# Re-ranking the planned order of a fused window-attention and two-MLP kernel, with one DRAM tile per later token block

## Chip, cores and metric

The kernel runs on one core of a Trainium2 chip. The metric is the device time of the launch in microseconds (us), lower is better; the times before are 829.63, 829.7 and 830.26 us, with a median of 829.7 us.

## What is computed

The inputs are q, k and v for 4 sequences of 576 tokens, 8 heads of 64; in all 2304 tokens of model width 512. Attention looks back over a window of 64 tokens. Two MLPs of inner width 2048 follow, the first with a squared relu, the second with a leaky relu.

```python
mask = (rel >= 0) & (rel < 64)
scores = np.where(mask, (1 / np.sqrt(D)) * (q @ k.T), -1e9)
x = softmax(scores) @ v                     # 2304 x 512
r = np.maximum(x @ moe_w_in, 0.0)
y = (s * (r * r) + b) @ moe_w_out           # 2304 x 512
h = y @ moe2_w_in
out = np.maximum(0.01 * h, h) @ moe2_w_out
```

## The kernel before

**Attention.** The tokens are 18 tiles of 128. Tiles 0 to 7 (the early ones, which feed token blocks 0 and 1) go through `add_attention`, tiles 8 to 17 through `add_later`. A later tile runs: load of q and k halves (`qk`, L241), load of v into a buffer `vs` of pool "big" (L247), scores on TensorE (`sc`, L272), ScalarE's copy of the scores into the same buffer (L337), the mask on VectorE (L346), a row maximum (L355, L358), eight exponentials on ScalarE (L363), normalising on VectorE (L369 to L372), a transpose on TensorE (`tp`, L378), its two copies on VectorE (L386, L390), the product with v on TensorE (`xps`, L403), a copy of each half to `pt` (ScalarE L412, VectorE L414), and a store of `pt` to the DRAM tile `xdr` (L568). The pool "big" holds two buffers.

**First MLP.** Tokens are cut into five blocks (four of 512, one of 256), the inner width into 16 chunks. A step is one block and one chunk: 12 matmuls `hps` (L680), then ScalarE's `r` (L692), VectorE's `r` (L694), ScalarE's `gh` (L697), VectorE's `gl` (L699), and 12 matmuls `acc` (L715) that add to four PSUM banks. Every fp32 operand is split into a high and a low part, so each product is three matmuls. The steps run as block 0 with chunks 0 to 7, block 1 with all chunks, block 0 with chunks 8 to 15, then blocks 2, 3 and 4. Where block 0 is finished, VectorE adds the sum stored earlier to each bank (`part`, L738) before the next block may use the bank. Blocks 2 to 4 read their x back from `xdr` (`xl`, L573) and split it (L578, L580). The weights of each chunk are rounded and split by ScalarE and VectorE (`add_weights`, L602 to L641).

**Second MLP.** It runs as seven products per pair of quarters instead of eight, over three blocks of 768 tokens (L1052). Its combined weights are made ahead, during the first MLP, in units u0, u1, ...: one load of 1 MB into a buffer `raw2` of the same pool "big" (L820), ScalarE's first copy into `flt2` (L602), VectorE's roundings (L604 to L616), sums (L847), low parts (L876, L868), ScalarE's high parts (L874, L866), and six stores to the DRAM tile `w1dr` (L884). The pool "tmp" of `flt2` and `pt` holds two buffers.

**The order.** Class `Order` plans the whole program before it is emitted. Each piece of work is given an engine, a reckoned time, a key, the pieces it follows, the buffers it takes and uses, and for a transfer a further `delay` until it counts as landed. Each engine takes the lowest key that is ready in the plan; the emitted order is then fixed, and on the chip each engine works through its own queue in that order and waits at the head of it. All the large loads and stores stand in SyncE's queue (SP). When a buffer is handed on, the next user waits for the transfers out of it. A step's keys are its number plus offsets; attention tiles, weight chunks and weight units have keys set by tables. Where the plan sees TensorE idle near the start, products of zeros are put in (`product_of_zeros`, L1284).

Of the kernel before, what the change touches and what calls it, by code (L numbers as in the profile page):

```python
# [9 lines left out]
F32 = mybir.dt.float32  # L10
# [5 lines left out]
P = 128  # L16
# [110 lines left out]
def kernel(  # L127
# [39 lines left out]
    xdr = dramp.tile([P, KD, T], F32, name="xdr")  # L167
# [37 lines left out]
    half = KF // 2  # L205
# [210 lines left out]
    def add_later(i, key):  # L416
# [9 lines left out]
        for g in range(2):  # L426
            add(name("sc", g), "pe", 480, key - 6, lambda g=g: scores(i, g, "t"),
# [3 lines left out]
        for r in range(2):  # L431
            add(name("tb", r), "act", 375, key - 5.7, lambda r=r: take_own(i, r),
                [name("sc", 1), name("both")], use=[("sc", i, r), ss])
            add(name("to", r), "dve", 660 if mask_of(i) else 330, key - 4.87, lambda r=r: take_before(i, r),
                [name("tb", r), ("masks",)], use=[("sc", i, r), ss])
# [5 lines left out]
        add(name("norm"), "dve", 1050, key - 3, lambda: normalise_all(i),  # L441
            [name("exp", h) for h in range(H)], use=[("sm", i), ss])
        add(name("tp"), "pe", 480, key - 2.96, lambda: transpose_all(i),
            [name("norm"), ("masks",)], [("t", "tp", i)], [ss])
        for n in range(2):
            add(name("tt", n), "dve", 640, key - 5.69, lambda n=n: part_keys(i, n),
# [5 lines left out]
        add(name("pv"), "pe", 1150, key - 1, lambda: values_all(i), [name("bank")],  # L452
            [("h", "xt", i, 1)], [("xt", i, 0), ss, pt])
        add(name("xo", 0), "act", 400, key - 5, lambda: leave_half(i, 0), [name("pv")],
            use=[("xt", i, 0), pt])
        add(name("xo", 1), "dve", 350, key - 5, lambda: leave_half(i, 1), [name("xo", 0)],
# [27 lines left out]
    def add_attention(i, b, t0, key):  # L484
# [12 lines left out]
        for n, room in enumerate((rq, rk)):  # L497
            add(name("lqk", n), "sp", 1000, key - 5.93, lambda n=n: load_qk(i, n),
                [name("lqk", 0)] if n else [], room, delay=1900)
        add(name("lv"), "sp", 1600, key - 2.25, lambda: load_v(i),  # L500
# [7 lines left out]
        for g in range(2):  # L508
            add(name("sc", g), "pe", 700, key - 5.82, lambda g=g: scores(i, g, sc),
# [5 lines left out]
            for j in range(4):  # L515
                add(name("mm", g, j), "dve", 172, key - 5.47, lambda g=g, j=j: mask_max(i, g, j),
                    [name("sc", g)] + ([name("mm", 0, 0)] if g + j else after_v) + [("masks",)],
                    first if g + j == 0 else (), [("sc", i, j % 2), ss, ("sm", i)])
                add(name("exp", g, j), "act", 390, key - 2.81, lambda g=g, j=j: exponent(i, g, j),
                    [name("mm", g, j)], use=[ss, ("sm", i)])  # L520

            if i < 2:
                add(name("inv", g), "dve", 360, key - 3.4, lambda g=g: invert(i, g, g + 1),
                    [name("exp", g, j) for j in range(4)], use=[("sm", i)])
            elif g == 0:
                add(name("inv", 0), "dve", 360, key - 3.4, lambda: invert(i, 0, 2),
# [891 lines left out]
```

## Time and profile before

| | us |
|---|---|
| median of three runs | 829.7 |
| the profiled execution | 827.88 |
| its span | 826.1 |
| TensorE busy in the span | 814.0 |
| VectorE busy | 624.0 |
| ScalarE busy | 414.6 |

The granted clock was 0.999 over the span (1.00 is the level of 2.4 GHz). All times of rows count from the start of the span. Attention and the first MLP take up to about 475 us, the second MLP the rest. A row of a timeline or of the chain begins with its start and its length; what stands in brackets is the idle time of the engine just before it and what ended that.

### The profile page before, as it was taken

How to read it: one execution, taken by the hardware profiler on the slowest of the kernel's cores; microseconds unless marked ns; L12 is line 12 of the kernel's file. 1: busy time of each engine (PE TensorE's matmuls, PEld its weight loads, DVE VectorE, ACT ScalarE, POOL GpSimd, SP SyncE). 2: the span in 40 equal slices, each digit the busy share in tenths (PEclk: the TensorE clock that was granted, in tenths of full speed). 3: DMA queues.
4: the chain of work that ended last, by engine and by line, in shares of the span. 5: the costliest groups of instructions: out<-in, count | busy, mean ns of one | idle time of the engine just before them, and what ended most of it. 6: DMA issues, size and time to landing. Idle time of an engine off the chain costs nothing.

```text
span 826.1 us, 14490 instructions
## 1 busy us (share of the span) xinstructions
PE 814.0 (99%) x5541; PEld 734.0 (89%) x5541; DVE 624.0 (76%) x1019; ACT 414.6 (50%) x880; POOL 4.5 (1%) x18
## 2 busy tenths in 40 slices
PE   8999999999989999999999999999999999999998
PEld 5778888888878887888889999999999999999998
DVE  6999997786877877778787857699366788455964
ACT  7999655355555454544446434256233365232443
POOL 2000000000000000000000000000000000000000
PEclk9999999999999999999999999999999999999999
DMA  8754543438666565657688399798887899878783
GB/s 327 282 190 145 168 170 131 140 109 274 185 238 201 201 218 162 217 181 235 212 279 281 127 315 353 257 322 279 292 268 257 269 304 306 272 253 262 254 265 112
DMA packets 84757, 192.32 MB, mean 233 GB/s; under 512 B 6992, under 2 KB 47952, under 8 KB 80720
## 3 DMA queue, kind: packets, MB, share of 16 engines
q1 hardware_dynamic: 84688, 191.39, 69.3%
q8 instruction: 44, 0.72, 0.4%
q14 instruction: 25, 0.20, 0.1%
HBM read 148.90 MB, written 42.47 MB: 232 GB/s over the span
## 4 chain that ended last, share of the span: by engine, by line
PE 90%; DVE 4%; ACT 2%; DMA 2%; issue 1%; ACTq 0%; SPq 0%
PE xps L1052 24%; PE acc L715 22%; PE hps L680 21%; PE zps L1052 12%; PE yps L1052 6%; PE sc L272 2%; PE xps L403 1%; PE warm L1284 1%; DMA w1dr<-raw 1%; DMA xdr<-pt 1%; DVE s L284 1%; DVE tmp L612 1%; ACT s L290 1%; DVE tmp L616 1%; PE xps L328 1%
## 5 line engine op out<-in xcount | busy, mean ns | idle before, releaser
L715 PE MATMUL acc<-gh,wh 128*128 128x512 f32 (+1 forms) x320 | 117.3, 372 | 1.2 <-ACT gh L697 1.2
L680 PE MATMUL hps<-xh,wh 128*128 128x512 f32 (+1 forms) x324 | 117.0, 368 | 0.5 <-ACT wh L635 0.5
L680 PE MATMUL hps<-xl,wh 128*128 128x512 f32 (+1 forms) x324 | 116.4, 367 | 0.0
L715 PE MATMUL acc<-gh,wl 128*128 128x512 f32 (+1 forms) x320 | 116.1, 368 | 0.0
L1052 PE MATMUL xps<-x2h,ws 128*128 128x384 f32 x384 | 105.8, 334 | 0.0
L952 DVE TENSOR_TENSOR g2s<-g,g2s 128x768 fp32r<-128x768 f32 x84 | 80.2, 955 | 29.6 <-ACT g2s L949 28.6
L1052 PE MATMUL xps<-g2s,ws 128*128 128x384 f32 x576 | 101.8, 334 | 0.0
L1075 ACT ACTIVATE part<-xps 128x384 f32<-128x384 f32 x90 | 43.9, 490 | 114.9 <-PE xps L1052 114.2
L1052 PEld LDWEIGHTS xps<-g2s,ws 128*128 128x128 f32 x576 | 100.0, 188 | 0.1
L949 ACT ACTIVATE g2s<-g 128x768 fp32r<-128x768 f32 x84 | 70.8, 847 | 58.1 <-PE xps L1052 37.5
L692 ACT ACTIVATE r<-hps 128x512 f32<-128x512 f32 (+1 forms) x80 | 44.4, 555 | 100.7 <-PE hps L680 100.2
L715 PE MATMUL acc<-gl,wh 128*128 128x512 f32 (+1 forms) x320 | 85.5, 371 | 0.0
L694 DVE SCALAR_TENSOR_TENSOR r<-r,sbt 128x512 f32<-128x512 f32 (+1 forms) x80 | 55.6, 695 | 36.0 <-ACT r L692 35.4
L680 PE MATMUL hps<-xh,wl 128*128 128x512 f32 (+1 forms) x324 | 79.7, 368 | 0.0
L697 ACT ACTIVATE gh<-r,sbt 128x512 fp32r<-128x512 f32 (+1 forms) x80 | 54.2, 677 | 37.4 <-DVE r L694 37.0
L680 PEld LDWEIGHTS hps<-xh,wh 128*128 128x128 f32 x324 | 61.1, 189 | 11.4 <-ACT wh L635 1.1
L715 PEld LDWEIGHTS acc<-gh,wh 128*128 128x128 f32 x320 | 60.3, 189 | 11.9 <-ACT gh L697 1.7
L680 PEld LDWEIGHTS hps<-xl,wh 128*128 128x128 f32 x324 | 61.1, 189 | 10.2 <-DVE xl L580 0.6
L1052 PEld LDWEIGHTS xps<-x2h,ws 128*128 128x128 f32 x384 | 70.1, 188 | 0.0
L715 PEld LDWEIGHTS acc<-gh,wl 128*128 128x128 f32 x320 | 60.4, 189 | 9.7
L699 DVE SCALAR_TENSOR_TENSOR gl<-r,sbt,gh 128x512 fp32r<-128x512 f32 (+1 forms) x80 | 55.5, 693 | 15.2 <-ACT gh L697 15.1
L715 PEld LDWEIGHTS acc<-gl,wh 128*128 128x128 f32 x320 | 56.7, 189 | 10.4 <-issue 0.7
(106 smaller groups left out, 1369.7 us busy)
## 6 DMA issues: line engine op xcount, KB each, us to landing
ws<-w1dr SPq DMA_DIRECT2D x84, 512.0 KB, 4.5
ws<-w2dr SPq DMA_DIRECT2D x84, 512.0 KB, 4.5
raw<-in_w SPq DMA_DIRECT2D x31, 1024.0 KB, 4.9
w1dr<-raw SPq DMA_DIRECT2D x16, 512.0 KB, 4.3
w2dr<-raw SPq DMA_DIRECT2D x16, 512.0 KB, 4.5
qk<-in_qk SPq DMA_DIRECT2D x20, 320.0 KB, 4.0
out<-st SPq DMA_DIRECT2D x24, 192.0 KB, 4.1
qk<-in_qe SPq DMA_DIRECT2D x16, 256.0 KB, 7.5
```

Of the source, the lines that this page charges most:

```text
L272: nc.tensor.matmul(out=sc_t[i][r][D * a:D * a + D, p, c0:c1], lhsT=qk_t[i, g][D * r:D * r + D, pp, D * a:D * a + D], rhs=qk_t[k, g][D * r: ...
L284: nc.vector.tensor_tensor_reduce(out=s_t[i][:, g, j, :], in0=sc_t[i][j % 2][:, 2 * g + j // 2, :], in1=mask[:, mask_of(i), :], scale=-SCAL ...
L680: nc.tensor.matmul(out=hps_t[s][:, c0:c1], lhsT=w[:, 0, kk * P:kk * P + P], rhs=x[l, b][:, kk, c0:c1], start=(kk == 0 and j == 0 and part ...
L692: nc.scalar.activation(out=r, in_=hps_t[s], func=ACTF.Relu)
L694: nc.vector.scalar_tensor_tensor(out=r, in0=r, scalar=sbt[:, 0:1], in1=r, op0=ALU.mult, op1=ALU.mult)
L697: nc.scalar.activation(out=gh, in_=r, func=ACTF.Identity, bias=sbt[:, 1:2])
L699: nc.vector.scalar_tensor_tensor(out=gl, in0=r, scalar=sbt[:, 1:2], in1=gh.bitcast(F32), op0=ALU.add, op1=ALU.subtract)
L715: nc.tensor.matmul(out=acc_t[r, m], lhsT=three[j][0], rhs=three[j][1], start=(c == c0 and j == 0), stop=(c == c1 - 1 and j == 2))
L949: nc.scalar.activation(out=out, in_=in_, func=ACTF.Copy)
L952: nc.vector.tensor_tensor(out=out, in0=in_, in1=hi.bitcast(F32), op=ALU.subtract)
L1052: nc.tensor.matmul(out=out, lhsT=w_[:, wcut], rhs=x_, start=(opens and j == k == 0), stop=(j == n - 1 and k == 2), skip_group_check=not opens)
L1075: nc.scalar.activation(out=t, in_=bank_t[(*key, "x")], func=ACTF.Copy)
```

## The change

Keys are set anew for the later tiles, the early tiles, the steps, the weight chunks and the weight units, most of them by small amounts. `xdr` becomes one DRAM tile for each of the blocks 2, 3 and 4, so the loads of x read contiguous rows. In the plan, a unit's buffers count as used for another 930 ns after each of its stores (a new piece of work named "gone" that emits nothing), and the wait ahead of a store is 200 instead of 500 ns. The first product of each later pair in the second MLP is given a rank 2.5 products earlier. The zero products start with 5 instead of 4 and end after step 5 instead of 7; their number, counted in the emitted order, is 49 in both kernels. `half` keeps its value of 8.

```diff
-    xdr = dramp.tile([P, KD, T], F32, name="xdr")
+    xdr = {b: dramp.tile([P, KD, n], F32, name=f"xdr{b}") for b, n in enumerate(BLOCKS1) if b > 1}
...
-            add(name("sc", g), "pe", 480, key - 6, lambda g=g: scores(i, g, "t"),
+            add(name("sc", g), "pe", 480, key - 7.32, lambda g=g: scores(i, g, "t"),
...
-        add(name("max"), "dve", 800, key - 4.87, lambda: row_max(i),
+        add(name("max"), "dve", 800, key - 11.33, lambda: row_max(i),
...
-            add(name("exp", h), "act", 330, key + 3, lambda h=h: exponent_row(i, h),
+            add(name("exp", h), "act", 330, key + 8.74, lambda h=h: exponent_row(i, h),
...
-        nc.sync.dma_start(out=xl[0, b][:, :, :n].bitcast(F32), in_=xdr[:, :, t0:t0 + n])
+        nc.sync.dma_start(out=xl[0, b][:, :, :n].bitcast(F32), in_=xdr[b])
...
-            [("x", *r) for r in x], delay=9000 if b > 2 else 4000)
+            [("x", *r) for r in x], delay=3785.46 if b > 2 else 6398.4)
...
-        add(("e", s, 3), "dve", 60 + 600 * f, s + (-0.76 if s < 8 else -0.9), lambda: activate(s, 3),
+        add(("e", s, 3), "dve", 60 + 600 * f, s + (-13.55 if s < 8 else 0.69), lambda: activate(s, 3),
...
-    DUE = 500
+    DUE = 200.0
...
+            add((*name(kind), "gone"), "none", 0, key, lambda: None, [name(kind)], use=[raw, flt],
+                delay=929.73)
...
+            at = key + (-2.5 if i == 1 and p else j) * ms
+            add(name("p", i), "pe", 6 * MM, at, lambda i=i: product1(b, p, i),
...
-    WARM, BETWEEN = 4, 13
+    WARM, BETWEEN = 5, 13
...
-    add(("fill", 1), "none", 0, 0, end_fill, [("e", KF // 2 - 1, 0)])
+    add(("fill", 1), "none", 0, 0, end_fill, [("e", 5, 0)])
...
-                key = first_step[0, 2] + -10.0 + 2 * (i - IN_W)
+                key = first_step[0, 2] + -10.14 + 2.09 * (i - IN_W)
...
-        add_weights2(u, STEPS1 + (1 if u[1] else -10) + 0.1 * n, after)
+        add_weights2(u, STEPS1 + (1.17 if u[1] else -8.65) + 0.1 * n, after)
```

Three places in the emitted order follow. The first is SP's queue around tile 13 (its v goes into `vs_2615` before, into `vs_2587` now); `raw2_2262` and `raw2_2305` are the buffer of unit u2, `flt2` its scratch. Before:

```order
L573 DMA xl_2519<-xdr_99 128x4x512
L884 DMA w1dr_100<-flt2_2372 128x2x256
L884 DMA w1dr_100<-flt2_2372 128x256
L884 DMA w1dr_100<-raw2_2262 128x4x256 x2
L247 DMA vs_2615<-in_vl 128x768
L241 DMA qk_2646<-in_qk 128x640
```

Now:

```order
L890 DMA w1dr_102<-raw2_2305 128x4x256
L247 DMA vs_2587<-in_vl 128x768
L241 DMA qk_2618<-in_qk 128x640
L567 DMA xdr3_100<-pt_2538 512x1x128
L890 DMA w1dr_102<-raw2_2305 128x4x256
L241 DMA qk_2659<-in_qk 128x640
```

Tile 13's load stood behind all of u2's stores and took u2's buffer; now it stands ahead of the last of them and takes the buffer of tile 12.

The second is SP's queue around tile 11, where `raw2_1911` is unit u1's buffer and `vs_2260` is tile 11's. Now:

```order
L890 DMA w1dr_102<-raw2_1911 128x4x256
L755 DMA ydr_98<-st_2188 128x512
L890 DMA w1dr_102<-raw2_1911 128x4x256
L755 DMA ydr_98<-st_2203 128x512
L755 DMA ydr_98<-st_2245 128x512
L247 DMA vs_2260<-in_vl 128x768
L241 DMA qk_2283<-in_qk 128x640
```

Before, the buffer that u1 leaves went to u2's load, and tile 11 followed that:

```order
L884 DMA w1dr_100<-raw2_1899 128x4x256 x2
L820 DMA raw2_2262<-in_w2 128x2048
L247 DMA vs_2302<-in_vl 128x768
L241 DMA qk_2334<-in_qk 128x640
L568 DMA xdr_99<-pt_2245 512x1x128
```

Tile 11 now takes the buffer that u1's last two stores leave.

The third is ScalarE's queue behind tile 17's product (`pt_3407`, now `pt_3410`), with the first copies `flt2` of units u5 and u6 among the `r` and `gh` of the steps. Before:

```order
L412 ACTIVATE pt_3407<-xps_3417 128x256
L602 ACTIVATE flt2_3468<-raw2_3409 128x1024
L692 ACTIVATE r_3481<-hps_3459 128x512
L602 ACTIVATE flt2_3495<-raw2_3456 128x1024
L697 ACTIVATE gh_3482<-r_3481,sbt_97 128x512
```

Now:

```order
L412 ACTIVATE pt_3410<-xps_3419 128x256
L698 ACTIVATE r_3479<-hps_3459 128x512
L608 ACTIVATE flt2_3484<-raw2_3456 128x1024
L703 ACTIVATE gh_3480<-r_3479,sbt_97 128x512
L698 ACTIVATE r_3511<-hps_3486 128x512
L608 ACTIVATE flt2_3516<-raw2_3473 128x1024
L703 ACTIVATE gh_3512<-r_3511,sbt_97 128x512
```

Each first copy moved back by about one step, u5's from ahead of the first `r` to behind it, and u6's from ahead of the first `gh` to ahead of the second.

## Rows read from the trace of the kernel before

**Rows 1.** The page's first part, busy time by engine.

```profile
PE 814.0 (99%) x5541; PEld 734.0 (89%) x5541; DVE 624.0 (76%) x1019; ACT 414.6 (50%) x880; POOL 4.5 (1%) x18
```

**Rows 2.** Stretches: length, PE, PEld, DVE, ACT, POOL busy, clock, DMA, GB/s.

```profile
0.00:20.00 20.00, 16.60 (x251) 10.34 (x252) 13.21 (x73) 14.19 (x55) 4.51 (x18) 1.00 0.88 326
20.00:50.00 30.00, 28.36 (x355) 22.56 (x354) 29.41 (x83) 27.94 (x82) 0.00 (x0) 1.00 0.71 266
50.00:90.00 40.00, 39.77 (x351) 32.18 (x350) 39.07 (x79) 36.01 (x88) 0.00 (x0) 1.00 0.42 148
90.00:135.00 45.00, 45.00 (x200) 37.26 (x199) 43.42 (x51) 23.71 (x30) 0.00 (x0) 1.00 0.46 157
...
225.00:260.00 35.00, 32.91 (x293) 26.45 (x292) 27.51 (x51) 18.45 (x57) 0.00 (x0) 1.00 0.66 223
...
475.00:593.00 118.00, 118.00 (x681) 117.67 (x680) 83.59 (x107) 49.29 (x78) 0.00 (x0) 1.00 0.91 305
```

**Rows 3.** TensorE's waits from 60 to 475 us: total, times, longest.

```profile
PE tp L378 <- DVE vs L372: 2.1, 1, 2.1
PE acc L715 <- ACT gh L697: 1.2, 1, 1.2
```

**Rows 4.** The chain that ended last, 215 to 245 us: start, length, what.

```profile
221.34 1.23 DVE raw L868
...
222.59 7.99 DMA w1dr<-raw
...
230.68 0.40 ACT vs L337
...
238.64 0.63 PE tp L378 x4
...
241.32 1.06 PE xps L403 x48
242.38 0.88 PE sc L272 x32
```

**Rows 5.** ScalarE's timeline at tile 13.

```profile
230.68 0.66 ACT L337 ACTIVATE vs<-sc 128x256 f32<-128x256 f32 x2 [3.15 <-DMA w1dr<-raw]
```

**Rows 6.** The chain that ended last, 296 to 314 us.

```profile
303.14 7.09 DMA xdr<-pt
...
310.39 0.07 ACT flt L602
...
311.40 0.72 ACT gh L697
```

**Rows 7.** ScalarE's timeline behind tile 17.

```profile
302.92 1.11 ACT L602 ACTIVATE flt<-raw 128x1024 f32<-128x1024 f32 x1
307.40 0.60 ACT L692 ACTIVATE r<-hps 128x512 f32<-128x512 f32 x1 [3.36 <-PE hps L680]
```

**Rows 8.** VectorE's timeline at u4's last low part and tile 17's normalising.

```profile
292.05 1.22 DVE L868 TENSOR_TENSOR raw<-raw 128x1024 f32<-128x1024 f32 x1
...
296.56 0.69 DVE L372 TENSOR_TENSOR vs<-vs,sum 128x512 f32<-128x512 f32 x1
```

**Rows 9.** The page's DMA issues, whole span: count, KB each, median us to landing.

```profile
w1dr<-raw SPq DMA_DIRECT2D x16, 512.0 KB, 4.3
```

**Rows 10.** DMA issues from 200 to 245 us.

```profile
w1dr<-raw SPq DMA_DIRECT2D x2, 512.0 KB, 8.0
raw<-in_w SPq DMA_DIRECT2D x1, 1024.0 KB, 7.3
```

**Rows 11.** DMA issues from 285 to 330 us.

```profile
raw<-in_w SPq DMA_DIRECT2D x3, 1024.0 KB, 5.5
```

**Rows 12.** VectorE's and TensorE's timelines at block 0's third bank.

```profile
248.82 0.68 DVE L738 TENSOR_TENSOR part<-acc,part 128x512 f32<-128x512 f32 x1
249.89 0.39 PE L715 MATMUL acc<-gh,wh 128*128 128x512 f32 x1
```

**Rows 13.** The page's costliest groups: busy, mean ns, idle before and its releaser.

```profile
L699 DVE SCALAR_TENSOR_TENSOR gl<-r,sbt,gh 128x512 fp32r<-128x512 f32 (+1 forms) x80 | 55.5, 693 | 15.2 <-ACT gh L697 15.1
```

More of the change, by code (lines that the diff above doesn't have):

```diff
@@ L497, in add_attention @@
         for n, room in enumerate((rq, rk)):
-            add(name("lqk", n), "sp", 1000, key - 5.93, lambda n=n: load_qk(i, n),
+            add(name("lqk", n), "sp", 1000, key + (-6.93 if early else -6.81), lambda n=n: load_qk(i, n),
                 [name("lqk", 0)] if n else [], room, delay=1900)
-        add(name("lv"), "sp", 1600, key - 2.25, lambda: load_v(i),
+        add(name("lv"), "sp", 1600, key + (-2.57 if early else 5.03), lambda: load_v(i),
             [("lw", 0, KF - 1, 0, 2)] if i == IN_W else
@@ L508, in add_attention @@
         for g in range(2):
-            add(name("sc", g), "pe", 700, key - 5.82, lambda g=g: scores(i, g, sc),
+            add(name("sc", g), "pe", 700, key + (-6.15 if early else -8.61), lambda g=g: scores(i, g, sc),
                 [("lqk", k, g) for k in (i, i - 1) if k >= 0]
@@ L535, in add_attention @@
                 for j in range(4):
-                    add(norm[j], "act", 305, key - 3, lambda g=g, j=j: normalise(i, g, j),
+                    add(norm[j], "act", 305, key - 3.77, lambda g=g, j=j: normalise(i, g, j),
                         [inv], use=[("sm", i), ss])
-            add(name("tp", g), "pe", 560, key - 9.17, lambda g=g: transpose_pe(i, g, tp),
+            add(name("tp", g), "pe", 560, key + (-13.47 if early else -9.62), lambda g=g: transpose_pe(i, g, tp),
                 norm + [("masks",)], [(tp, "tp", i, g)], [ss])
-            add(name("tt", g), "act", 478, key - 12.62, lambda g=g: take_transposed(i, g),
+            add(name("tt", g), "act", 478, key + (-7.19 if early else -0.48), lambda g=g: take_transposed(i, g),
                 [name("tp", g)] + ([name("tt", 0)] if g else []),
@@ L543, in add_attention @@
             last = [name("tt", g)]
-            add(name("pv", g), "pe", 620, key - 1.6, lambda g=g: values(i, g, xt),
+            add(name("pv", g), "pe", 620, key + (-1.29 if early else 1.7), lambda g=g: values(i, g, xt),
                 last + [name("lv")] + ([name("pv", 0)] if g else []),
@@ L552, in add_attention @@
             return
-        add(name("xh"), "act", 478, key - 0.73, lambda: split_x_hi(i, b, t0),
+        add(name("xh"), "act", 478, key + (4.88 if early else -6.68), lambda: split_x_hi(i, b, t0),
             [name("pv", 0), name("pv", 1)] + ([("xh", i - t0 // P)] if t0 else []),
@@ L556, in add_attention, with to_block @@
             [("xt", i), ("xh", 0, b), ("xl", 0, b)])
-        add(name("xl"), "dve", 602, key + 0.73, lambda: split_x_lo(i, b, t0),
+        add(name("xl"), "dve", 602, key + (-0.76 if early else 2.53), lambda: split_x_lo(i, b, t0),
             [name("xh")], use=[("xt", i), ("xh", 0, b), ("xl", 0, b)])
     xo_t = {}
+    def to_block(i, t):
+        b = i * P // NMAX
+        c = i * P - sum(BLOCKS1[:b])
+        nc.sync.dma_start(out=xdr[b][:, :, c:c + P], in_=t)
     def leave_x(i):
@@ L567, in store_x @@
     def store_x(i):
-        nc.sync.dma_start(out=xdr[:, :, i * P:i * P + P], in_=xo_t[i])
+        to_block(i, xo_t[i])
     def load_x(b):
@@ L656, in add_weights @@
             add(("cv", *a, part), "dve" if part else "act",
-                (70, 220, 220, 160, 160)[part] + n * (490, 200, 200, 490, 490)[part], key,
+                (70, 220, 220, 160, 160)[part] + n * (490, 200, 200, 490, 490)[part], key + ((2.25, -0.11, 7.57, -0.45, -2.38)[part] if c < 8 else 0),
                 lambda part=part: float_w(*a, part),
@@ L893, in add_weights2 @@
         name = lambda kind, *a: (kind, *u, *a)
-        add(name("lw2"), "sp", 3200, key, lambda: load_w2(u), after, [("big", *raw)], delay=1900)
+        add(name("lw2"), "sp", 3200, key, lambda: load_w2(u), after, [("big", *raw)], delay=1834.43)
         for part in range(5):
```

55 lines of the change are left out of this document (27 added, 28 removed).

## Prediction

> **What bounds the kernel now.** I read the engines' busy times first. TensorE is busy for 814.0 of the 826.1 us of the span [rows 1], so nothing but TensorE's own work and its 12.1 us of idle time can shrink. The change takes no product away and adds none: the emitted orders hold the same matmuls and the same 49 products of zeros. The gain is therefore bounded by idle time that goes, and the loss by idle time that comes.
>
> The stretches then say where the idle time lies [rows 2]. The second MLP has none (118.00 busy of 118.00; the stretches up to its tail read alike), so the moved first product of a pair can win nothing there, and its weights' transfers already keep up. The last 3.4 us are the tail behind the last matmul, which the change leaves as it is. From 90 to 135 us TensorE is busy for 45.00 of 45.00. The front, 20 to 90 us, has 1.64 + 0.23 = 1.87 us of idle time, and there VectorE is nearly as full as TensorE (29.41 of 30 and 39.07 of 40).
>
> TensorE's list of waits from 60 to 475 us has just two entries [rows 3]: one transpose of a later tile that waited 2.1 us for VectorE's normalising, and one `acc` that waited 1.2 us for `gh`. Together 2.09 + 1.25 = 3.34 us in the finer record. These are what the change can remove. The granted clock reads 1.00 in each stretch of rows 2 and I see nothing here to change it.
>
> **First wait: tile 13.** The chain [rows 4] goes from u2's last low part (VectorE, 221.34, 1.23 us long) to its store, 7.99 us, and only then to ScalarE's copy of tile 13's scores at 230.68, which had idled for 3.15 us on that store [rows 5]. The copy writes into the buffer that u2 had left. It was wanted at 230.68 - 3.15 = 227.53, so 4.9 us after the store's issue at 222.59; 3.15 us late on ScalarE became 2.09 on TensorE. In the new order tile 13's load stands ahead of u2's last store and takes tile 12's buffer, whose readers are VectorE and TensorE, long done. There are also 56 matmuls between tile 13's scores and its transpose instead of 40. I take the whole 2.09 us as gone.
>
> **Second wait: u6's first copy.** ScalarE's `flt` at 310.39 waited for tile 17's store, 7.09 us long from 303.14, with `gh` queued behind it until 311.40 [rows 6]; `acc` waits for that `gh`. Now that copy stands one step further back, behind the second `r`, some 4.5 us later in TensorE's work (12 `hps` and 8 `acc` at 45.00 / 200 = 0.225 us each [rows 2]). The store would have landed well before. This takes 1.25 us off, if nothing else comes late at the same place.
>
> Something could. Ahead of the same `gh` there now stands u5's first copy, which needs its 1 MB load, which needs the buffer that u4's last store leaves. That store depends on a low part on VectorE that ran at 292.05 before, and now stands just behind tile 17's normalising, which ended at 296.56 + 0.69 = 297.25 [rows 8]. So: 297.25 + 1.2 = 298.5 issue; 4.3 us for the store [rows 9] gives 302.8; 5.5 for the load [rows 11] gives 308.3. The copy can start once `r` is done at 307.40 + 0.60 = 308.0 [rows 7]; for no wait at all it must start by 312.17 - 1.25 (when TensorE wanted `gh`) - 0.76 (`gh` itself) - 1.01 (the copy) = 309.1. With the worst of the rows, 8.0 for the store and 7.3 for the load [rows 10], the load lands at 313.8, and the wait would be 4.7 us. Before, the same unit's copy ran at 302.92 with no wait for its load [rows 7], so the short times are the nearer ones. I take 0, and 0 to 4.7 as the bounds.
>
> **New buffer for tile 11.** Tile 11 now takes the buffer that u1's stores leave, as tile 13 did with u2's. Counting from tile 10's transpose: the last store goes out behind a copy of a bank to `st`, about 3.0 us later; the copy of tile 11's scores is wanted after 0.63 of transpose, 24 matmuls (5.4 us), and the product and scores together 1.06 + 0.88 [rows 2, 4], about 8.0. That is a head start of 5.0 to 5.2 us, hardly more than the 4.9 which failed in rows 4. If the store takes 4.3 us [rows 9], nothing waits; if it takes 8.0 [rows 10], the copy is 2.8 us late. 41 matmuls between scores and transpose (9.2 us) leave 1.5 to 2.0 us over the 7.3 to 7.8 that the softmax takes, so TensorE would wait 0.8 to 1.3. Tile 9's and 14's windows shrink from 10.0 to 8.2 us, which costs 0 to 0.9 by the same softmax. I take 0.2 us for tile 11, nearer to 0 since its stores are spread by two stores of y, and 0.2 for the other two.
>
> The Trainium skill (DMA: Bandwidth & Descriptors, section "Anatomy of one DMA — SWDGE (gpsimd) path") gives a DMA's time as some 2.0 us plus its bytes at 436 GB/s, for the path by GpSimd; as an estimate that is 3.2 us for 512 KB. By it tile 11 never waits and the total is 0.2 us lower; but by it tile 13 would not have waited in the kernel before either, and rows 4 show 7.99. With other transfers in flight the measurement decides.
>
> **Block 0's end.** The third bank's `acc` stands 8 matmuls (1.8 us) earlier against tile 13, since two blocks of `hps` no longer separate the banks. Before, VectorE freed that bank at 248.82 + 0.68 = 249.50, and `acc` came at 249.89 [rows 12]: 0.4 us to spare. VectorE's first additions stand earlier now too, ahead of a unit's roundings, so I take 0.2 us, with 0 and 1.8 - 0.4 = 1.4 as the bounds.
>
> **Front, x and the rest.** In VectorE's order, the work ahead of each weight chunk's low part, each `gl` and each `xl` sums to nearly the same time in both orders, and both orders meet again at the end of block 0's first run. I take 0, with 0.6 us to either side. The contiguous loads of x stand at the same places behind the same stores and TensorE did not wait for x: 0.
>
> **Sum.** -2.09 - 1.25 + 0 + 0.2 + 0.2 + 0.2 + 0 = -2.7 us. The profiled execution of 827.88 would become 825.2 and its span 823.4. The median of the runs, 1.8 us above that execution, would become 829.7 - 2.7 = 827.0.
>
> **Rivals.**
>
> *The waits only move.* Tile 11 waits like tile 13 did (1.3 us instead of 0.2), and u5's load comes 1.0 to 1.5 us late ahead of `gh`. For it speaks that a 512 KB store took 8.0 us beside other stores [rows 10] and that tile 11's head start is no longer than tile 13's; against it, the median of 4.3 [rows 9]. It gives 827.0 + 1.1 + 1.2 = 829.3, from 828.1 to 830.5.
>
> *The front gets shorter as well.* TensorE's 1.87 us of idle time between 20 and 90 us, or part of it, goes since the early tiles' chains are better spread, and the four small costs above stay away. Against it: VectorE is full there [rows 2]. It gives 829.7 - 3.3 - 1.5 = 824.9.
>
> *VectorE waits in the front.* For steps 0 to 7 `gl` is ranked 13 steps ahead, so it heads VectorE's queue as soon as `gh` is near, and roundings of the next chunk queue behind it. VectorE has 0.59 + 0.93 us to spare from 20 to 90 us [rows 2], so what it waits more there is paid by TensorE. Each `gl` waits 15.1 / 80 = 0.19 us for `gh` on average [rows 13]. It makes the kernel slower than before beyond what can be told once it adds more than 2.7 + 1.66 = 4.4 us, 0.55 us for each of the eight steps; at 0.75 us each it is 6.0 us and 833.0. Against it: by the sums of VectorE's order `gl` is not nearer to its `gh` in most of these steps.
>
> **How the numbers follow.** A measurement of this kernel can tell about 0.2%, 1.66 us: below 828.0 is faster, above 831.4 slower. The forecast has 0.46 (826.2 to 828.3, of which 0.42 faster and 0.04 the same), the moved waits 0.26 (the same), the shorter front 0.14 (faster), VectorE's waits or u5's load at the end of its bounds 0.14 (slower). That makes faster 0.56, the same 0.30, slower 0.14. The range from 824.7 to 831.0 holds the first two cases, most of the third, and leaves out the slower case and the edge of the third, about 0.18.
>
> **What would show it.** Right: no wait of tile 13's transpose on L372, tile 13's score copy with no DMA as its releaser, `acc` not waiting for `gh` behind tile 17, the span at 823 to 824. The moved waits show as a score copy of tile 11 that a store `w1dr<-raw` released, or as u5's first copy released by `raw<-in_w`. VectorE's waits show as TensorE busy for less than 28 of the 30 us from 20 to 50, or less than 39 of 40 from 50 to 90. The forecast is wrong if any wait of over 1 us stands in TensorE's list from 60 to 475 us, or if the second MLP has idle time.

## Result and profile after

The kernel after takes 822.24 us (median of 5 runs, 821.53 to 824.57), the kernel before 829.63 us in the same set (5 runs, 828.82 to 830.26): a ratio of 0.9917, 95% interval 0.9901 to 0.9933, or 7.4 us less. The forecast was 827.0 with a range from 824.7 to 831.0, so the sign was right and the size was not.

The profiled execution of after took 822.12 us, its span 820.3. The page's engine line and its chain of waits, by engine:

```profile
PE 813.8 (99%) x5541; PEld 733.7 (89%) x5541; DVE 623.7 (76%) x1019; ACT 413.8 (50%) x880; POOL 4.5 (1%) x18
...
PE 95%; DVE 2%; ACT 1%; DMA 1%; issue 0%; SPq 0%
```

TensorE does the same 5541 matmuls in the same time as in [rows 1]; its idle time fell from 12.1 to 820.3 - 813.8 = 6.5 us. The stretches, with the columns of [rows 2], say where:

```profile
0.00:20.00 20.00, 18.34 (x260) 10.70 (x260) 14.14 (x78) 15.10 (x61) 4.50 (x18) 1.00 0.87 331
20.00:50.00 30.00, 28.69 (x400) 23.72 (x399) 29.69 (x95) 29.04 (x85) 0.00 (x0) 1.00 0.71 266
50.00:90.00 40.00, 40.00 (x308) 32.17 (x307) 39.11 (x65) 33.25 (x81) 0.00 (x0) 1.00 0.46 161
...
180.00:225.00 45.00, 45.00 (x417) 36.98 (x416) 34.64 (x62) 25.11 (x71) 0.00 (x0) 1.00 0.69 222
225.00:260.00 35.00, 35.00 (x301) 28.78 (x300) 27.58 (x50) 18.08 (x56) 0.00 (x0) 1.00 0.61 204
260.00:312.00 52.00, 52.00 (x420) 42.70 (x419) 37.80 (x64) 27.50 (x80) 0.00 (x0) 1.00 0.53 181
475.00:593.00 118.00, 117.96 (x681) 117.58 (x680) 81.12 (x103) 48.89 (x77) 0.00 (x0) 1.00 0.90 306
```

TensorE has no idle time left at the later tiles in this execution: 35.00 of 35.00 from 225 to 260 us, where [rows 2] had 32.91, and 52.00 of 52.00 behind them. The forecast's 2.09 us at tile 13 and its 1.25 behind tile 17 are gone. A further part went where the forecast had put nothing: idle time up to 20 us is 1.66 instead of 3.40 us, and from 20 to 90 us 1.31 instead of 1.87. Together that is 2.3 us in this pair of traces; the other traces, under "The front" below, give less.

TensorE's list of waits over the whole span, all entries that it shows (what waited, for whom: total, times, longest), is now

```profile
PE warm L1295 <- DVE zeros L1315: 1.1, 1, 1.1
PE sc L272 <- DMA qk<-in_qe: 0.5, 2, 0.4
PE tp L311 <- ACT pt L317: 0.5, 1, 0.5
PE xps L328 <- DVE nmax L284: 0.4, 1, 0.4
PE xps L328 <- ACT pt L317: 0.3, 1, 0.3
```

Both entries of [rows 3] are gone, and all that is left lies in the first 40 us.

At tile 13 the timelines of VectorE and TensorE show the normalising finished at 231.09 and the transpose at 233.01, with no idle time ahead of it, so 1.9 us to spare:

```profile
230.40 0.69 DVE L372 TENSOR_TENSOR vs<-vs,sum 128x512 f32<-128x512 f32 x1
233.01 0.60 PE L378 MATMUL tp<-ident,vs 128*128 128x128 f32 x4
```

Tile 11, which now takes the buffer that u1 leaves, and the first copies of u5 and u6 behind tile 17, in ScalarE's timeline, against [rows 5] and [rows 7]:

```profile
191.26 0.66 ACT L337 ACTIVATE vs<-sc 128x256 f32<-128x256 f32 x2
...
303.16 1.12 ACT L608 ACTIVATE flt<-raw 128x1024 f32<-128x1024 f32 x1
...
306.78 1.14 ACT L608 ACTIVATE flt<-raw 128x1024 f32<-128x1024 f32 x1
```

None has a bracket, so none waited.

One wait on a store did come in, at a place that the forecast had not looked at. ScalarE's high part of u2 (L872, which is L866 before) waits for a store of u2, with `gh` and tile 12's copy to `pt` queued behind it:

```profile
217.46 1.06 ACT L872 ACTIVATE raw<-raw 128x1024 fp32r<-128x1024 f32 x1 [1.70 <-DMA w1dr<-raw]
```

The two traces of before have no such wait; the seven traces with the new ranks of the later tiles and the longer hold on the units' buffers (three of after, four of the experiments) all do, from 1.6 to 3.2 us. In five of them TensorE loses nothing by it. In the two others it does, 0.8 us in a kernel of the experiments and 0.7 us in the third trace of the kernel after:

```profile
221.75 0.50 PE L686 MATMUL hps<-xh,wh 128*128 128x512 f32 x1 [0.67 <-ACT pt L412]
```

u1's stores landed after 3.4 us (DMA issues from 172 to 205 us), the two of 280 to 320 us after 3.0, where [rows 10] had 8.0 for u2's:

```profile
w1dr<-raw SPq DMA_DIRECT2D x2, 512.0 KB, 3.4
```
```profile
w1dr<-raw SPq DMA_DIRECT2D x2, 512.0 KB, 3.0
```

With these two the estimate of 3.2 us, which the prediction drew from the Trainium skill (DMA: Bandwidth & Descriptors, "Anatomy of one DMA — SWDGE (gpsimd) path") for another path, agrees. In [rows 10] and in the runs below the same 512 KB took 4.4 to 8.9 us beside other transfers.

### The profile page after: what moved, and what is told of

The parts are those of the page before. It is cut to its first block, busy times and chain, and to the rows that moved or that the text cites. A ratio compares the mean times of both kernels' runs of the same rounds, so it can differ in the third digit from the quotient of the medians.

```text
span 820.3 us, 14486 instructions
## 1 busy us (share of the span) xinstructions
PE 813.8 (99%) x5541; PEld 733.7 (89%) x5541; DVE 623.7 (76%) x1019; ACT 413.8 (50%) x880; POOL 4.5 (1%) x18
## 4 chain that ended last, share of the span: by engine, by line
PE 95%; DVE 2%; ACT 1%; DMA 1%; issue 0%; SPq 0%
PE acc L721 24%; PE xps L1061 24%; PE hps L686 24%; PE zps L1061 12%; PE yps L1061 6%; PE sc L272 2%; PE xps L403 1%; DMA qk<-in_qe 1%; PE xps L328 1%; PE tp L378 1%; DVE s L304 0%; ACT s L290 0%; PE tp L311 0%; DVE s L284 0%; ACT s L301 0%
```

## Experiments

Each was timed in turns with the kernel before on the same chip. Medians of before were 827.19 us (20 runs, first set), 827.25 (29, second), 827.52 (26, third) and 826.88 (11, fourth).

### The kernel before once more

> The kernel before, unchanged, for a second trace. The profiled execution of 827.88 us lay 1.75 us under the median of the timed ones. Theory: its two waits on transfers (tile 13's transpose 2.09 us, u6's copy ahead of gh 1.25 us) and the front's idle time differ from execution to execution, so a second trace shows the same two entries in TensorE's list from 60 to 475 us with other lengths, and the span follows: about 826 + (their sum - 3.34) + (front's idle - 5.3). Rival: the waits repeat within 0.3 us and a longer span comes from elsewhere (the first microseconds, the tail or the second MLP).

One execution of 826.41 us, span 824.7. TensorE's waits:

```profile
PE tp L378 <- DVE vs L372: 1.6, 1, 1.6
PE acc L715 <- ACT gh L697: 1.2, 1, 1.2
```

The waits of [rows 3] belong to the kernel, not to one execution, though their length varies: 2.8 us here, 3.3 there. The idle time of the first 90 us varies more, 3.9 us here and 5.3 there; with these two the expected sum gives a span of 824.1, near the 824.7 measured. The kernel before itself took 825.45 to 830.46 us in this set; the three runs that the prediction started from (829.63 to 830.26) lie at the upper end of that.

### The front's ranks alone, and all others alone

The kernel before with the ranks of tiles 0 to 7, of the first eight weight chunks and steps, and the filler of zero products:

```diff
-            add(name("sc", g), "pe", 700, key - 5.82, lambda g=g: scores(i, g, sc),
+            add(name("sc", g), "pe", 700, key + (-6.15 if early else -8.61), lambda g=g: scores(i, g, sc),
...
-        add(("e", s, 3), "dve", 60 + 600 * f, s + (-0.76 if s < 8 else -0.9), lambda: activate(s, 3),
+        add(("e", s, 3), "dve", 60 + 600 * f, s + (-13.55 if s < 8 else -0.9), lambda: activate(s, 3),
...
-    WARM, BETWEEN = 4, 13
+    WARM, BETWEEN = 5, 13
```

> The kernel before with only the front's new ranks: tiles 0 to 7, weight chunks 0 to 7, steps 0 to 7, the zero products' start and end. From 90 us on its order is that of before. Theory (the front was mis-sized, parts add): TensorE's idle time from 0 to 90 us falls from 5.3 to 3.0 us, first hps at 30.4 instead of 31.5 us, and the two later waits stay: 2.3 us under before, some 827.3. Rival (the front's gain is eaten by VectorE, full there): 829 to 830, with idle time that comes back behind 60 us.

825.36 us (10 runs) against 827.19; ratio 0.9973 [0.996, 0.9986], so 1.8 us less. The two later waits stayed (2.1 and 1.4). This gain comes from the front alone.

The other half, everything but that:

```diff
-    xdr = dramp.tile([P, KD, T], F32, name="xdr")
+    xdr = {b: dramp.tile([P, KD, n], F32, name=f"xdr{b}") for b, n in enumerate(BLOCKS1) if b > 1}
...
-            add(name("sc", g), "pe", 480, key - 6, lambda g=g: scores(i, g, "t"),
+            add(name("sc", g), "pe", 480, key - 7.32, lambda g=g: scores(i, g, "t"),
...
-    DUE = 500
+    DUE = 200.0
```

> The kernel before with all the change except the front's ranks: later tiles, steps from 8 on, weight units, DRAM tiles by block, the pairs' first products. Its order around tiles 11 to 17 is that of the changed kernel. Theory: the two waits go, the front stays: 3.3 us under before by the traces, up to 5.1 if the 1.75 us between the profiled execution and the median of before were longer waits at the same places: 824.5 to 826.3. Rival (the new order moves them to tile 11 and to u5's copy): 828 to 829, with an entry for tp or acc of 1 us or more in TensorE's list.

824.18 us (5 runs) against 827.19; ratio 0.9964 [0.9951, 0.9977], 3.0 us less, and neither `tp` of a later tile nor `acc` in the list of waits. 1.8 + 3.0 = 4.8 us: the halves add up to less than the first result of 7.4.

The profile of the front's kernel fell on its longest execution, 828.59 us, and shows a cost that no term of the sum had. These are stretches of 2 us at tile 13 (columns as in [rows 2]):

```profile
234.00:236.00 2.00, 1.97 (x8) 1.09 (x7) 1.14 (x2) 2.00 (x12) 0.00 (x0) 1.00 1.03 350
236.00:238.00 2.00, 0.00 (x0) 0.00 (x0) 1.73 (x4) 1.23 (x6) 0.00 (x0) 1.00 1.06 431
238.00:240.00 2.00, 1.93 (x7) 1.73 (x8) 0.96 (x2) 0.00 (x0) 0.00 (x0) 0.57 0.51 209
240.00:242.00 2.00, 2.00 (x7) 1.51 (x5) 2.00 (x4) 1.79 (x2) 0.00 (x0) 0.58 0.00 0
242.00:244.00 2.00, 2.00 (x78) 1.72 (x80) 1.43 (x4) 0.38 (x1) 0.00 (x0) 1.00 0.35 131
```

TensorE stands still from 236 to 238 us, waiting for tile 13, and right behind that the granted clock is 0.57 for four microseconds, nearer to the 1.2 GHz level than to that of 2.4. At 1 - 0.575 for 4 us this costs about 1.7 us; TensorE's busy time in that execution was 816.1 us, 2.1 more than in [rows 1]. In this execution the wait cost more than its own length.

### One load in the front

The prediction's trace had VectorE idle for 0.78 us at 17.18 us, waiting for a copy that waited for the second half of a weight load. The load was issued two places earlier on SP, all else the same:

```diff
+MOVES = [(('lw', 0, 0, 1, 2), ('lqk', 2, 1))]
```

> The kernel before with one transfer moved: the load of the second half of weight chunk 0 is issued ahead of the second q/k half of tile 2, two places earlier in SP's queue; no other engine's order changes. Theory (the front gained as VectorE no longer waited 0.78 us at 17.18 us for this load's first copy): that wait goes, first hps comes 0.5 to 0.9 us earlier, the time falls by as much: 828.7 to 829.1. Rival (what counts is VectorE's own order, tiles' row maxima ahead of the roundings): no change, or up to 0.7 us longer since tile 2's and 3's scores get their q and k later.

829.37 us (10 runs) against 827.19; ratio 1.0014 [0.9998, 1.0031]: no gain that can be told. Six of the ten executions had a mean clock of 0.997 or 0.998 and took 829.3 to 830.3 us; the four others took 825.5 to 826.8, with a median of 826.2 against 826.6 for before's executions above 0.998. VectorE's idle time went, but TensorE's timeline shows a price, a wait for the `qk` that now stood behind:

```profile
13.92 1.42 PE L281 MATMUL sc<-qk 64*64 64x64 f32 x57 [1.19 <-DMA qk<-in_qe]
```

So the least gain that was expected, 0.5 us, can't be excluded for an execution at full clock, but the front's 1.8 us don't come from this idle time of VectorE alone.

### The kernel after once more, and the pause filled

> The changed kernel, unchanged, beside the kernel before on one chip. In the runs so far the kernel before lay between 825.5 and 830.5 us, those with a mean granted clock of 0.997 or 0.998 from 827.9 on, those with 1.000 from 825.5 to 827.7. Theory: a TensorE pause of about 2 us is followed, in some executions, by some microseconds at the lower clock level; the changed kernel has no such pause, so none of its runs shows 0.997, its times spread over less than 3 us, and it is 5.5 us under the before of the same chip (3.3 for the two waits' own length, 2.2 for the front), more only as far as before shows lowered clocks. Rival: the 7.4 us hold on any chip, with or without lowered clocks in before.

823.12 us (821.82 to 824.89, 6 runs) against 827.25 (825.21 to 830.45, 29 runs); ratio 0.994 [0.9918, 0.9962]. The change is worth 4.1 us here by the medians and 5.0 by the ratio, less than the 5.5 expected, and no execution of it has a mean clock under 0.999.

Does the lowered clock behind the pauses explain the rest? Two versions of before fill the pauses with products of zeros, so that TensorE hardly stops there:

```diff
+        if i == 13:
+            product_of_zeros(acc_t[2, 3], 9)
```

> The kernel before with nine products of zeros (about 1.9 us) put just ahead of tile 13's transpose, so TensorE works through most of the wait instead of pausing; nothing else changes. Theory (the pause lowers the clock afterwards): the wait itself stays paid, the runs at 0.997 to 0.998 go or become rare, the median falls to the level of before's runs at 1.000, about 826.3, up to 3 us under a before that has many lowered runs. Rival (the lowered clock has nothing to do with that pause): the same share of lowered runs and the same median as before, within 0.5 us.

and besides

```diff
+        if s == 42 and m == 0 and 0 in parts:
+            product_of_zeros(acc_t[r, 3], 5)
```

> As the one with nine products, and five more ahead of the acc that waits for u6's first copy behind tile 17 (1.25 us). Theory (only the long pause matters): the same as with nine alone, within 0.5 us. Rival (the shorter pause lowers the clock in some executions too): fewer runs at 0.998 than with nine alone, and a further 0.5 to 1.5 us.

827.86 us (12 runs) and 827.02 us (12 runs) against 827.25; ratios 0.9999 and 0.9992. The waits were covered: nine products took 2.12 us ahead of the transpose, which then had no idle time.

```profile
237.61 2.12 PE L1286 MATMUL acc<-zeros 128*128 128x512 bf16 x9
239.56 0.60 PE L380 MATMUL tp<-ident,vs 128*128 128x128 f32 x4
```

A mean clock of 0.998 or less showed in 3 of these 24 executions, against 27 of the 86 of before in the four sets. But the median did not fall, and the means were 827.8 and 827.1 us against 827.6. Part of this may be the products themselves: VectorE's normalising ended at 239.14 us here, 0.4 us before the transpose, which stood behind the products, started.

The profiled execution with nine products is one of the three, and in it the clock fell somewhere else, behind a wait of 1.0 us in the front that the kernel before has too (1.57 us in the prediction's trace, with the clock at 1.00 behind it):

```profile
15.93 0.62 PE L272 MATMUL sc<-qk 64*64 64x64 f32 x15 [1.02 <-issue]
18.00:20.00 2.00, 2.00 (x6) 0.69 (x5) 1.97 (x13) 1.89 (x10) 0.00 (x0) 0.50 1.02 397
```

So tile 13 is not the only place at which before can lose its clock.

The other way round, the kernel after with a pause made at tile 13, by 20 matmuls that now stand behind its transpose instead of ahead of it:

```diff
+MOVES = [(('y', 30, 0), ('h', 32, 1, 0)), (('y', 30, 1), ('h', 32, 1, 0)), (('h', 32, 0, 0), ('h', 32, 1, 0))]
```

> The changed kernel with the order of TensorE alone altered at tile 13: its transpose stands 20 matmuls earlier (12 acc and 8 hps now follow it), so TensorE reaches it at about 228.5 us and has to wait for VectorE's normalising at 231.1, a pause of 2.6 us that the kernel before had in like form. Theory: 2.6 us are lost in every run, and in some the clock falls behind the pause for 3 to 4 us, which costs 1.5 to 2 more: median 2.6 to 4.5 us above the changed kernel, with two groups of runs. Rival (a pause costs its length only): 2.4 to 2.8 us above, one group, no run at 0.997.

826.86 us (12 runs) against 823.12 for the kernel after: 3.7 us for a wait of 2.6. Its longest wait, and stretches of 2 us, of which the first two hold the pause:

```profile
PE tp L387 <- DVE vs L381: 2.6, 1, 2.6
```
```profile
228.00:230.00 2.00, 0.53 (x3) 0.11 (x1) 0.80 (x2) 1.15 (x6) 0.00 (x0) 1.00 0.98 334
230.00:232.00 2.00, 0.86 (x5) 0.89 (x6) 1.59 (x4) 0.77 (x2) 0.00 (x0) 0.85 0.57 238
232.00:234.00 2.00, 2.00 (x7) 1.52 (x6) 1.38 (x2) 1.10 (x1) 0.00 (x0) 0.50 0.00 0
234.00:236.00 2.00, 2.00 (x9) 1.60 (x8) 0.00 (x0) 0.00 (x0) 0.00 (x0) 0.80 0.03 8
```

8 of its 12 executions had a mean clock of 0.997 or 0.998; of the 17 of after in the first result and the sets here, one had (in the fourth set). So this pause brings the lowered clock. In the traced execution it cost 1 - 0.85, 1 - 0.50 and 1 - 0.80 of 2 us each, together 1.7 us. In the medians that price is not shown as clearly: the four executions at 1.0 took 826.5 us and the eight lowered ones 827.1, and the former already lie 3.4 us above after for a wait of 2.6. In before the lowered clock comes in about every third execution.

### The parts of the later half

The plan's longer hold on the units' buffers alone:

```diff
-    DUE = 500
+    DUE = 200.0
...
+            add((*name(kind), "gone"), "none", 0, key, lambda: None, [name(kind)], use=[raw, flt],
+                delay=929.73)
```

> The kernel before with only the plan's new reckoning of the weight units' transfers (buffers held 930 ns longer after each store, 200 instead of 500 ns ahead of it, the load's delay 1834 instead of 1900). In its emitted order tile 13 still takes the buffer of unit u2, and u6's first copy no longer stands ahead of the gh that waited. Theory (each wait hangs on its own place in the order): tile 13's wait stays at 1.3 to 2.1 us, the wait for gh behind tile 17 goes: 1.2 us under before. Rival (the longer hold alone is what the change lives on): both waits go, 3 us under before.

833.18 us (5 runs) against 827.52; ratio 1.0065 [1.0031, 1.01], 5.7 us slower. Tile 13's wait stays and new ones arise:

```profile
PE tp L378 <- DVE vs L372: 2.1, 1, 2.1
PE zps L1055 <- DVE raw L868: 1.8, 1, 1.8
PE xps L1055 <- DMA ws<-w1dr: 1.3, 3, 0.7
...
PE xps L1055 <- DVE g2s L955: 1.0, 1, 1.0
```

The units come later, and the second MLP, whose weights they make, waits for 1.8 + 1.3 = 3.1 us on these weights and 1.0 us besides. TensorE's busy time in this trace is 816.5 us, 2.5 more than in [rows 1] at a clock of 1.00; that part is not explained. The prediction's "its weights' transfers already keep up" holds for the whole change, and not for this part of it.

The ranks of tiles 8 to 17 alone (13 lines, among them those below), then both together:

```diff
-        add(name("max"), "dve", 800, key - 4.87, lambda: row_max(i),
+        add(name("max"), "dve", 800, key - 11.33, lambda: row_max(i),
...
-            add(name("exp", h), "act", 330, key + 3, lambda h=h: exponent_row(i, h),
+            add(name("exp", h), "act", 330, key + 8.74, lambda h=h: exponent_row(i, h),
```

> The kernel before with only the new ranks of tiles 8 to 17. Tile 13 still takes u2's buffer, 1 unit's first copy has left the place behind tile 17. Theory: tile 13's wait stays, since its buffer's stores are still issued late; the other goes: 1 to 1.5 us under before. Rival (56 instead of 40 matmuls between tile 13's scores and its transpose cover the late store): both go, 3 us under before.

> The new ranks of tiles 8 to 17 and the new reckoning of the units' transfers together, nothing else. Now tile 13 takes tile 12's buffer. Theory: both waits go, as with all the later parts together: 3.0 us under before, within 0.7. Rival (the steps' ranks, the loads of x and the DRAM tiles by block are needed too): 1 to 2 us under before, with a wait of 1 us or more left in TensorE's list.

825.35 us (10 runs), ratio 0.9975 [0.9959, 0.999], and 824.07 us (10 runs), ratio 0.9962 [0.995, 0.9975], against 827.52. By the ranks alone `acc` no longer waits. Tile 13 still takes u2's buffer, and ScalarE's copy of its scores still waits for u2's store, 1.67 us instead of 3.15; with 44 matmuls between its scores and its transpose, which starts at 231.38 us, that no longer reaches TensorE. The one wait of a transpose that the list has is tile 14's:

```profile
222.53 0.66 ACT L337 ACTIVATE vs<-sc 128x256 f32<-128x256 f32 x2 [1.67 <-DMA w1dr<-raw]
247.56 0.63 PE L378 MATMUL tp<-ident,vs 128*128 128x128 f32 x4 [0.83 <-DVE vs L372]
```

With both, tile 13 takes tile 12's buffer, and no transpose of a later tile and no `acc` is in the list. This pair carries the later half's gain: 3.45 us against 3.0 for the whole half.

The DRAM tiles of x and the pairs' first products alone:

```diff
-        nc.sync.dma_start(out=xl[0, b][:, :, :n].bitcast(F32), in_=xdr[:, :, t0:t0 + n])
+        nc.sync.dma_start(out=xl[0, b][:, :, :n].bitcast(F32), in_=xdr[b])
...
-            add(name("p", i), "pe", 6 * MM, key + j * ms, lambda i=i: product1(b, p, i),
+            at = key + (-2.5 if i == 1 and p else j) * ms
+            add(name("p", i), "pe", 6 * MM, at, lambda i=i: product1(b, p, i),
```

> The kernel before with only one DRAM tile for each later block and the pairs' first products ranked earlier. Theory: 0, within 0.6 us, both waits and the front as before; the load of x for block 2 lands in 5 to 8.7 us as before. Rival (contiguous rows land 2 to 4 us sooner and relieve the stores that run beside them): tile 13's wait shrinks by 1 us or more and the time with it.

825.59 us (10 runs) against 827.52; ratio 0.9986 [0.9967, 1.0004], unclear. In its one profile the load of x landed after 6.5 us and u2's stores beside it after 5.8, where before's second profile had 8.5 and 7.3, and tile 13 waited for only 0.2 us. That speaks for the rival of this run. So the layout was undone in the kernel after, whose emitted order this leaves as it is:

```diff
-    xdr = {b: dramp.tile([P, KD, n], F32, name=f"xdr{b}") for b, n in enumerate(BLOCKS1) if b > 1}
+    xdr = dramp.tile([P, KD, T], F32, name="xdr")
```

> The kernel after with x of the later blocks kept in one DRAM tile again: the emitted order is word for word that of the kernel after, only the loads of x read four rows of 2 KB per partition again instead of one of 8 KB. Theory (the contiguous load relieves the stores beside it): the two stores of unit u2 beside the load of x land after 6.9 to 8.4 us again instead of 5.3, the load itself after 8 to 9 instead of 5.8; since tile 13 takes another buffer in this order, little of it reaches TensorE: 0 to 0.5 us slower than the kernel after on the same chip. Rival (a good part of the gain of the later order hangs on the layout): a wait of the later tiles or of gh comes back between 170 and 320 us and it is 1 to 2.5 us slower than the kernel after. Second rival (the layout does nothing): the load takes 5.8 as before.

> The kernel after once more, beside the three others on one chip, as their upper mark. If the 7.4 us of the first result are the change's: 819.8 to 821 with before at 827.5. If 4.1 to 5.0 us are, and the rest belonged to the executions of before on the first chip: 822.5 to 823.4 with before at 827.5.

822.26 us (5 runs) with one tile and 823.32 us (6 runs) for the kernel after, against 826.88 (11 runs); ratios 0.9938 [0.9923, 0.9953] and 0.9951 [0.9935, 0.9968]. In the kernel after the layout gains nothing that shows. Whether it shortens transfers, this pair does not tell; the DMA issues from 205 to 250 us of the kernel with one tile, and then of after in this set:

```profile
xl<-xdr SPq DMA_DIRECT2D x1, 1024.0 KB, 7.2
w1dr<-raw SPq DMA_DIRECT2D x2, 512.0 KB, 5.0
```
```profile
xl<-xdr SPq DMA_DIRECT2D x1, 1024.0 KB, 7.5
w1dr<-raw SPq DMA_DIRECT2D x2, 512.0 KB, 4.4
```

The contiguous load took 7.5 us here, 5.8 in after's first profile. The other traces say more. In the order of before, seven traces with the one tile (two of before, those of the front's ranks, the moved load, the two filled ones and the longer hold) had 8.2 to 9.7 us for the load and 6.9 to 8.4 for u2's stores; the one with the tiles by block had 6.5 and 5.8. In the order of after, or with the ranks of tiles 8 to 17, the one tile took 7.1 to 7.2 us in three traces, and the tiles by block 5.8 to 7.5 in five, four of them under 6.4. So the load most likely does land sooner by block, though two traces with half of the front's ranks (next) had 6.7 and 5.3 with the one tile. And tile 13's wait in the order of before goes with u2's stores: 0.2 us where they took 5.8; 1.3, 1.6, 2.1, 2.1, 2.1 where they took 6.9, 7.3, 7.9, 8.0, 8.4. In that order the layout may thus be worth something; in the order of after tile 13 no longer hangs on these stores. And after's gain here is 3.6 to 4.1 us, again not 7.4.

The first products of the pairs were not run by themselves. With the later half they are in a kernel that gained 3.0 us, without them the ranks and the hold gained 3.45, so no gain of theirs shows.

### The parts of the front

The ranks of tiles 0 to 7 and of their keys alone (16 lines, among them)

```diff
-            add(name("tt", g), "act", 478, key - 12.62, lambda g=g: take_transposed(i, g),
+            add(name("tt", g), "act", 478, key + (-7.19 if early else -0.48), lambda g=g: take_transposed(i, g),
```

> The kernel before with only the ranks of tiles 0 to 7 and the ranks of their keys. Theory A (the front's gain comes from the early tiles' own chains): idle time of TensorE behind the first hps falls from 1.0 us to about 0.3, and the time is 1.5 to 2 us under before's. Theory B (the gain comes from when the weight chunks and the gl of the first steps are made): no gain, within 0.5 us of before. Theory C (the parts are only good together): slower than before by more than 1 us. The two later waits stay, 3.0 us together.

and those of the chunks, the steps and the filler alone (among them)

```diff
-            add_weights(0, c, 1, 2, -10.9, -7.78)
+            add_weights(0, c, 1, 2, -15.39, -7.67)
...
-    add(("fill", 1), "none", 0, 0, end_fill, [("e", KF // 2 - 1, 0)])
+    add(("fill", 1), "none", 0, 0, end_fill, [("e", 5, 0)])
```

> The kernel before with only the ranks of the first eight weight chunks and of the first eight steps, and the five zero products more of the filler. Theory A (early tiles): no gain, within 0.5 us of before. Theory B (chunks and steps): 1.5 to 2 us under before's. Theory C (only good together): slower by more than 1 us, with waits of sc or tp for VectorE between 0 and 90 us. The two later waits stay.

834.62 us (4 runs), ratio 1.009 [1.0072, 1.0108], and 834.18 us (6 runs), ratio 1.0075 [1.0054, 1.0097], against 826.88. Each part alone costs 7 to 8 us, both together gain 1.8: they are only good together. Of the list of waits of the tiles' kernel, and then of the chunks' kernel, these are the longest:

```profile
PE sc L272 <- DVE xl L473: 2.4, 1, 2.4
```
```profile
PE sc L272 <- issue: 2.5, 2, 2.1
PE acc L715 <- DVE part L738: 2.1, 1, 2.1
PE hps L680 <- ACT wh L635: 2.0, 3, 0.9
```

The page's groups show a second price, the filler, which puts products of zeros where the plan has a gap (columns: busy, mean ns, idle before). First the tiles' kernel, then the chunks':

```profile
L1284 PE MATMUL warm<-zeros 128*128 128x512 bf16 x54 | 14.9, 421 | 1.1 <-DVE zeros L1304 1.1
L1284 PE MATMUL acc<-zeros 128*128 128x512 bf16 x6 | 1.5, 379 | 0.0
```
```profile
L1284 PE MATMUL warm<-zeros 128*128 128x512 bf16 x52 | 14.7, 432 | 1.1 <-DVE zeros L1304 1.1
L1284 PE MATMUL acc<-zeros 128*128 128x512 bf16 x12 | 2.9, 381 | 0.0
```

They run 60 and 64 of these where before and after run 49, 11.9 + 0.8 = 12.7 us of them in before: 3.7 and 4.9 us more. The chunks' kernel got fifteen more of them, where five had been expected. Its granted clock was 0.91 over the first 20 us besides, 1.8 us, and the two cover its 820.4 - 814.0 = 6.4 us of added busy time. In the tiles' kernel it was 0.96 from 90 to 135 us, another 1.8, and some 3 us of the 8.6 added stay unexplained.

## Why the prediction was wrong in size and right in sign

**The two waits: right.** -2.09 and -1.25 were forecast. Both entries are gone, and by the paths named: tile 13's load takes another buffer and its transpose has 56 matmuls behind its scores; u6's copy finds its buffer free. The later half alone measured -3.0, the ranks with the hold on the buffers -3.45. That the ranks cover most of tile 13's late store without the other buffer, at the price of a wait at tile 14, and that the hold alone loses, was not seen.

**What was added for new waits: wrong, by 0.6.** Tile 11 (+0.2), tiles 9 and 14 (+0.2) and block 0's third bank (+0.2) all measured nothing. u1's store took 3.4 us; the 8.0 of [rows 10], which I let weigh on it, was the duration of u2's store beside a load of x. (Tile 11's room, 9.2 less 7.3 to 7.8, was 1.4 to 1.9 us and not 1.5 to 2.0; nothing hung on it.) u5's copy was put at 0 and was 0. The new wait that did come, ScalarE's on u2's store at 217 us, was in no term; it reached TensorE in two traces of seven, with 0.7 and 0.8 us, so the rival of the moved waits was right that one moves, but not in where, nor in that it costs 2.3 us.

**The front: the failed step of the sum.** "I take 0, with 0.6 us to either side" measured -1.8 in the run with the front's ranks alone. I read the term from VectorE's order, as sums of work ahead of a few instructions, and VectorE was nearly full. The account of TensorE's idle time also left out the first 20 us: [rows 2] have 20.00 - 16.60 = 3.40 us there, and I named only the 1.87 from 20 to 90 us. The gain lies in TensorE's short waits. Behind the first `hps` they were 0.31 + 0.27 + 0.22 + 0.23 = 1.03 us in before's timeline and are one of 0.28 in after's:

```profile
39.00 1.17 PE L328 MATMUL xps<-pt,vt 128*64 128x64 f32 x32 [0.28 <-ACT pt L317]
```

Gone are a wait of the scores `sc` and two of `hps` for ScalarE's high part of the weights. That part repeats: nine traces of kernels with before's front have 0.98 to 1.31 us there (one has 2.13), six with after's 0.28 (one has 0.47). Ahead of the first `hps` single profiles can't size the gain: its start lies between 29.96 and 33.79 us in the nine and between 29.88 and 31.14 in the six. Up to 90 us the nine have 3.6 to 6.2 us of idle time in all, with a median of 4.1, and the six 2.5 to 3.8, with a median of 2.9. So 1.2 us of the 1.8 can be seen as idle time, 0.75 of it behind the first `hps`; the 2.3 of the first pair of traces was in part luck, since the prediction's trace was one of the worst of its nine. In two of the nine the clock fell in the front besides, in none of the six. The rival of a shorter front had this sign and a price of 1.5; I gave it 0.14. The rival in which VectorE waits was on the other side; a loss of that size came only when one half of the front's ranks was taken without the other, and then much of it was zero products. Which of the ranks do it together stays open.

**Loads of x: right for this change.** 0 forecast, and the kernel after with one tile again is as fast.

**The base: the other failed step.** The sum was made against an execution of 827.88 us and then moved up by 1.8 to the median of three runs, 829.7. In the four later sets before's median was 826.9 to 827.5, and of 86 runs 8 were at or above 829.63; after's three medians were 822.2, 823.1 and 823.3. So 827.88 was the better base. From it, -3.34 for the waits and -1.8 for the front give 822.7, where after is. The three failed terms, 0.6 for new waits, 1.8 for the front and 1.8 for the base, are 4.2 of the 4.8 us by which 827.0 missed. What set the first runs of before 2.4 us higher stays open; the lowered clock is a candidate, since before's runs at 0.998 or less have a median of 828.8 and the others 826.7, but the clock of those first runs is not on record.

**The clock: a term that was missing.** "I see nothing here to change it" was true of the profiled execution. In about a third of before's executions the mean clock is lower, and these are about 2 us longer (medians of 828.8 and 826.7), which by estimate is some 0.7 us in the mean. The runs don't confirm that sum: with the pauses filled the lowered executions became rare and the mean stayed.

## What to carry to other kernels

A median of three runs and one profiled execution can differ by more than a term of the sum, and the choice between them, here 1.8 us, has to be given a range of its own. A table of ranks that was set jointly has no parts that can be priced singly: three of its parts lost 5.7 to 7.7 us alone and gained beside the others. And in a full front the sum of an engine's work says little; list the bound engine's short waits one by one, from its first instruction on and over more than one trace, and count the filler among its work.

## What the runs showed of the hardware

In six of the traces the granted clock fell behind a standstill of TensorE: at tile 13 behind 2.1 and 2.6 us (the front's ranks alone, and the pause made at tile 13), at 98 us behind 2.4 (the early tiles' ranks alone), and at 16 to 22 us, in the front, behind 1.0, 1.8 and 2.1 (nine products, the DRAM tiles with the pairs' first products, the chunks' and steps' ranks). Stretches of 2 us behind it read from 0.50 to 0.96, then 1.00 again, and by them each fall cost 1.7 us. The same standstill in another execution did not bring it: before's own trace has 2.1 us at tile 13 and 1.57 in the front at 1.00 throughout. The Trainium skill (TensorE: Matmul & The Clock Gate, "Part 1: The HAM clock gate") says that the lowered level is the state at rest and that activity lifts it, and the rows at 236 to 244 us above agree: down behind the standstill, back to 1.00 under load. Which executions it strikes, no run here shows.

Landings of one transfer differ between executions by more than many edits do: u2's stores of 512 KB took 8.0 and 7.3 us in two executions of before, 5.3 and 4.4 in two of after.
